# A spectral mixing and feed-forward kernel: its opening in a new order (w_in's first piece first, two products of w_in behind the last transform, w_out converted ahead of the first unit)

## Chip, cores, metric

One Trainium2 chip, one core of it. The metric is the device time of one launch in microseconds, median of several executions; lower is better. The runs were made in four sittings, on more than one chip, so kernels are compared by their ratio to the kernel before in the same sitting. The granted clock is the share of its full clock that TensorE was allowed in a stretch; "warm" stands for 1.00 and "cold" for 0.50. Engine names in the profile: PE is TensorE (matmul), PEld its weight loads, DVE is VectorE, ACT is ScalarE, POOL is GpSimd, SP is SyncE, which here issues DMAs only.

## The reference, cut to what matters

```python
x: (8, 3136, 256) float32
X = np.fft.fft(np.fft.fft(x, axis=1), axis=2).real       # mixing, over sequence and features
x = X.reshape(25088, 256)
h = x @ w_in                                             # 256 -> 1024
solu = h * softmax(h)
ln = (solu - mean) / sqrt(var + 1e-6) * g_ln
out = ln @ w_out                                         # 1024 -> 256
```

The weights arrive in float64 (eight bytes a number), so the kernel converts them itself, with integer operations on VectorE.

## The kernel before: the parts that matter here

The batch is worked off in four pairs. The first transform of a pair runs over pieces c = 0 to 7: two loads (xa straight, xb mirrored by an indirect DMA), an addition of the mirror and a fold on VectorE, four matmuls, a copy to z on ScalarE, a store of z to DRAM (zd). The turn reads zd back in another arrangement as g. Then 25 units per pair follow: a second transform, the up-product with w_in (L207), softmax work on VectorE and ScalarE, a block transpose, and four units later the down-product with w_out (L291). While a pair's units run, the next pair is loaded and transformed beside them. Only the first pair has nothing to hide behind: that is the opening.

```python
def turn(pr, i):
    pr.g[i] = gpool.tile([P, KG, D], FP32, tag="g", name="g")
    for j in range(4):
        k = j * NK + i * KG
        nc.gpsimd.dma_start(out=pr.g[i][j * NH : (j + 1) * NH, :, :],
                            in_=pr.zd[k : k + KG, :, :].rearrange("k n d -> n k d"))

# ... in Weights:
def load_out(self):                      # eight loads of 256 KB, float64
    ...
    for c in range(KF):
        load_piece(moe_w_out, self.raw[:, 2 * c * D : 2 * (c + 1) * D], Wo[:, c], c, 0, D)
    nc.vector.tensor_scalar(out=g_ln, in0=g_ln, scalar1=2.0 ** -20, scalar2=None, op0=ALU.mult)

def narrow_out(self, i):                 # a quarter of w_out to float32, times g_ln
    ...

def centre(self):                        # takes the mean over the 1024 rows out of w_out
    ...
    nc.scalar.mul(out=wbar, in_=cs, mul=1.0 / FF)
    for c in range(KF):
        nc.gpsimd.tensor_tensor(out=Wo[:, c, :], in0=Wo[:, c, :], in1=wbar, op=ALU.subtract)

def ahead(pr, step):                     # the next pair, beside unit `step`
    c, r = divmod(step - 2, 2)
    if step == 0:
        load(pr, 0)
        load(pr, 1)
    elif 0 <= c < NC:
        if r == 0:
            add_mirror(pr, c, nc.gpsimd)
        else:
            fold(pr, c)
            ...

# ... the opening:
for c in range(NC):
    add_mirror(first, c, nc.vector)
    fold(first, c)
    ...                                  # loads of later pieces
    for s in range(CH // 2):
        transform1(first, c * CH // 2 + s)
    if c < 4:
        weights.narrow_in(c)
    ...
    elif 3 < c < 7:
        weights.product_in(c - 4)
    if c == 5:
        weights.load_out()
weights.place_table()
turn(first, 0)
for i in range(2):
    weights.narrow_out(i)

# ... at the end of each unit i:
    if i < 2:
        weights.narrow_out(i + 2)
    elif i == 2:
        weights.centre()
    if 0 < i + 1 < NK // KG:
        turn(first, i + 1)
    if ahd:
        ahead(ahd, cur.k1)
```

The program's order is each engine's order: nothing is rearranged behind it.

## Time and profile before

| | us |
|---|---|
| median of the first 3 executions (of 4) | 1255.19 (1254.85) |
| the profiled execution, its span | 1256.66, 1254.8 |
| first product of the second transform (unit 0 begins) | 77.41 |
| first vector instruction of unit 0 ("even", L213) | 83.17 |
| first matmul after TensorE's last large gap (here called T) | 135.08 |
| TensorE busy from T to the end | all of it, but for 3 us near the end |

How to read it: TensorE has no slack after T, so all that the opening can do is to move T. The prediction below shows the lines for this.

### The profile page before, as it was taken

Reading aid. Unit: us, or ns where it says so; the run is one execution under the profiler, and the core shown is the slowest. Engines: PE = TensorE matmul, PEld = TensorE weight load, DVE = VectorE, ACT = ScalarE, POOL = GpSimd, SP = SyncE. Lnnn points to the kernel's source line nnn. Section 1 sums busy time; section 2 is a strip of 40 time slices with the busy share of each in tenths; the row PEclk is TensorE's granted clock in tenths of the full one; section 3 lists DMA queues with packets and bytes.
Section 4 is the critical chain, followed back from the end, with each engine's and each line's share of the span. In section 5 each row is a group of like instructions: output and inputs, shape, how many; then the busy total and the mean of one; then the engine's idle time right before and its main releaser. Section 6 shows DMA issues by size and latency. Waiting matters only on the chain.

```text
span 1254.8 us, 15771 instructions
## 1 busy us (share of the span) xinstructions
PE 1181.9 (94%) x4864; PEld 897.2 (72%) x4864; DVE 930.4 (74%) x1383; ACT 613.0 (49%) x1151; POOL 541.5 (43%) x964
## 2 busy tenths in 40 slices
PE   2746799999999999999999999999999999999997
PEld 1423587777777777877877778778777777777786
DVE  6748877877776887777776887787676787777760
ACT  1223554555554555545454555455454555555551
POOL 2014755444553555444453554553453333333331
PEclk9677899999999999999999999999999999999999
DMA  9636787675798676774697678866878464555643
GB/s 234 209 98 131 155 177 161 155 168 135 143 183 180 141 181 160 165 171 104 155 194 179 136 176 172 166 154 139 154 161 159 98 138 111 128 124 115 132 101 99
DMA packets 461971, 189.52 MB, mean 151 GB/s; under 512 B 430166, under 2 KB 443742, under 8 KB 461888
## 3 DMA queue, kind: packets, MB, share of 16 engines
q1 hardware_dynamic: 448064, 149.96, 56.8%
q0 software_dynamic: 13824, 38.55, 11.7%
q8 instruction: 40, 0.66, 0.2%
q14 instruction: 43, 0.35, 0.1%
HBM read 44.78 MB, written 38.80 MB: 67 GB/s over the span
## 4 chain that ended last, share of the span: by engine, by line
PE 89%; DVE 5%; DMA 2%; issue 1%; POOL 1%; ACT 1%; POOLq 0%; DVEq 0%; ACTq 0%; SPq 0%
PE ps_o L291 54%; PE ps_h L207 26%; PE ps L158 4%; PE ps L181 3%; PE ps L183 1%; DMA xb<-in_x_dram,idx 1%; DVE tmp L329 1%; POOL Wo L425 1%; DMA xa<-in_x_dram 0%; DVE h L221 0%; DVE tmp L342 0%; DVE u L240 0%; DMA raw_out<-in_moe_w_out_dram 0%; PE wps L403 0%; DVE y L119 0%
## 5 line engine op out<-in xcount | busy, mean ns | idle before, releaser
L291 PE MATMUL ps_o<-Wo,uT 128*128 128x256 f32 x3136 | 699.8, 381 | 2.9 <-DMA out_dram<-ot 2.9
L291 PEld LDWEIGHTS ps_o<-Wo,uT 128*128 128x128 f32 x3136 | 612.9, 197 | 66.0 <-issue 3.7
L207 PE MATMUL ps_h<-Wi,q 128*128 128x512 f32 x800 | 367.5, 603 | 12.7 <-DVE ev L213 11.8
L240 DVE SCALAR_TENSOR_TENSOR u<-h,u 128x1024 f32<-128x1024 f32 x196 | 233.6, 1228 | 140.0 <-ACT u L232 140.0
L232 ACT ACTIVATE u<-h,neg 128x1024 f32<-128x1024 f32 x196 | 223.5, 1141 | 205.4 <-DVE neg L226 192.2
L242 POOL TENSOR_SCALAR nmean<-usum 128x1 f32<-128x1 f32 x196 | 127.0, 649 | 385.0 <-DVE u L240 384.8
L249 ACT ACTIVATE h<-u,nmean 128x1024 f32<-128x1024 f32 x196 | 223.6, 1142 | 129.8 <-POOL nmean L242 129.8
L207 PEld LDWEIGHTS ps_h<-Wi,q 128*128 128x128 f32 x800 | 154.5, 194 | 165.6 <-issue 156.0
L221 DVE CUSTOM_DVE_ANT_0 h<-ev,ps_h 128x1024 f32<-128x1024 f32 x196 | 231.8, 1219 | 47.4 <-PE ps_h L207 39.5
L276 DVE STREAM_TRANSPOSE v<-u 128x1024 f32<-128x1024 f32 x200 | 238.1, 1231 | 0.1
L213 DVE SCALAR_TENSOR_TENSOR ev<-w_mid,q,ps_h 128x1024 f32<-128x1024 f32 x100 | 127.8, 1278 | 76.0 <-PE ps_h L207 72.7
L189 ACT COPY q<-ps 128x257 f32<-128x257 f32 x100 | 37.4, 374 | 219.4 <-PE ps L183 133.7
L303 POOL DMA_INDIRECT out_dram<-ot,idx x96 | 102.7, 1070 | 46.3 <-issue 22.4
L158 PE MATMUL ps<-y,F 98*100 98x258 f32 (+3 forms) x288 | 79.1, 411 | 36.3 <-DVE y L120 36.3
L181 PEld LDWEIGHTS ps<-T,g 128*128 128x128 f32 x400 | 60.7, 192 | 60.0 <-issue 60.0
L261 POOL TENSOR_SCALAR v<-ssq 128x2 f32<-128x2 f32 (+1 forms) x100 | 27.1, 271 | 169.4 <-ACT h L249 169.4
L296 ACT ACTIVATE ot<-ps_o,rs 128x256 f32<-128x256 f32 x196 | 80.9, 457 | 30.6 <-PE ps_o L291 30.6
L158 PEld LDWEIGHTS ps<-y,F 98*100 98x100 f32 x288 | 46.3, 184 | 50.7 <-DVE y L120 27.1
L264 POOL TENSOR_TENSOR rs<-v,neg_half 128x2 f32<-128x2 f32 (+1 forms) x100 | 72.4, 724 | 7.8
L181 PE MATMUL ps<-T,g 128*128 128x128 f32 x400 | 61.3, 276 | 12.4 <-DMA g<-zd 12.4
L170 POOL DMA_DIRECT2D g<-zd x80 | 48.0, 606 | 57.1 <-DMA xa<-in_x_dram 49.4
L161 ACT COPY z<-ps 100x512 f32<-100x512 f32 x64 | 36.2, 569 | 41.8 <-PE ps L158 26.8
(60 smaller groups left out, 480.6 us busy)
## 6 DMA issues: line engine op xcount, KB each, us to landing
uT<-v SPq DMA_DIRECT2D x784, 128.0 KB
zd<-z SPq DMA_DIRECT2D x32, 400.0 KB
g<-zd POOLq DMA_DIRECT2D x80, 160.0 KB, 5.5
out_dram<-ot SPq DMA_DIRECT2D x100, 128.0 KB
xa<-in_x_dram SPq DMA_DIRECT2D x28, 392.0 KB
raw_in<-in_moe_w_in_dram SPq DMA_DIRECT2D x4, 512.0 KB
raw_out<-in_moe_w_out_dram SPq DMA_DIRECT2D x8, 256.0 KB
uT<-v SPq DMA_DIRECT2D x32, 64.0 KB
```

Of the source, the lines that this page charges most:

```text
L158: nc.tensor.matmul(o[..., cs], F[:, 2 * t + h, :], i[..., cs], start=first, stop=True, skip_group_check=True)
L181: nc.tensor.matmul(ps[:, h * P : (h + 1) * P], g[:, k, h * P : (h + 1) * P], T[:, k1, :], start=(h == 0), stop=True, skip_group_check=True)
L207: nc.tensor.matmul(ps[:, fs], t.q[:, c * P : (c + 1) * P], Wi[:, c, fs], start=True, stop=True)
L213: nc.vector.scalar_tensor_tensor(out=t.ev, in0=w_mid, scalar=t.q[:, KD * P :], in1=ps, op0=ALU.mult, op1=ALU.add)
L221: nc.vector.tensor_tensor_reduce(out=t.h[s], in0=t.ev, in1=ps, scale=1.0, scalar=-3.0e38, op0=ALU.subtract if s else ALU.add, op1=ALU.max, ...
L232: nc.scalar.activation(out=t.u[s], in_=t.h[s], func=ACT.Exp, bias=t.neg[:, s : s + 1], accum_out=t.esum[:, s : s + 1])
L240: nc.vector.scalar_tensor_tensor(out=t.u[s], in0=t.h[s], scalar=1.0, in1=t.u[s], op0=ALU.mult, op1=ALU.mult, accum_out=t.usum[:, s : s + 1])
L242: nc.gpsimd.tensor_scalar(out=t.nmean[:, s : s + 1], in0=t.usum[:, s : s + 1], scalar1=-1.0 / FF, scalar2=None, op0=ALU.mult)
L249: nc.scalar.activation(out=t.h[s], in_=t.u[s], func=ACT.Square, bias=t.nmean[:, s : s + 1], accum_out=t.ssq[:, s : s + 1])
L276: nc.vector.transpose(out=t.batch.v[:, t.w, :, o], in_=t.u[s])
L291: nc.tensor.matmul(ps, uT[:, c, :, s], Wo[:, c, :], start=(c == 0), stop=(c == KF - 1))
L303: dma = nc.gpsimd.indirect_dma_start(out=out, out_offset=bass.IndirectOffsetOnAxis(ap=idx[:, i : i + 1], axis=0), in_=t.ot[s], in_offset=None)
```

## The change

Its intent is a shorter opening. VectorE idles for 8.6 us at the start; a conversion of w_in is put there. Two of three products of w_in go into the time in which z is stored and turned. w_out is loaded in one transfer and earlier, all four quarters of it are converted before unit 0, and its mean is taken out by one instruction on VectorE after unit 1 instead of eight on GpSimd after unit 2. The first turn is issued half by SyncE and half by GpSimd.

```diff
-    def turn(pr, i):
+    def turn(pr, i, engines=(nc.gpsimd,) * 4):
...
-            nc.gpsimd.dma_start(out=pr.g[i][j * NH : (j + 1) * NH, :, :],
+            engines[j].dma_start(out=pr.g[i][j * NH : (j + 1) * NH, :, :],
...
-            for c in range(KF):
-                load_piece(moe_w_out, self.raw[:, 2 * c * D : 2 * (c + 1) * D], Wo[:, c], c, 0, D)
+            if moe_w_out.dtype == FP32:
+                ...
+            else:
+                nc.sync.dma_start(out=self.raw.rearrange("p (c f) -> p c f", c=KF),
+                                  in_=moe_w_out.bitcast(I32).rearrange("(c p) f -> p c f", p=P))
...
-            for c in range(KF):
-                nc.gpsimd.tensor_tensor(out=Wo[:, c, :], in0=Wo[:, c, :], in1=wbar, op=ALU.subtract)
+            nc.vector.tensor_tensor(out=Wo, in0=Wo, in1=wbar.unsqueeze(1).to_broadcast([P, KF, D]), op=ALU.subtract)
...
+        weights.load_in()
+        weights.piece_in(0)
         load(first, 0)
         nc.sync.dma_start(out=F, in_=f_tab)
-        weights.load_in()
-        weights.piece_in(0)
         for c in range(1, 4):
+            weights.piece_in(c)
             load(first, c, rooms.get(c))
-            weights.piece_in(c)
-        weights.load_tables()
         for c in range(4, 6):
             load(first, c, rooms[c])
+        weights.load_tables()
...
         for c in range(NC):
+            if c < 4:
+                weights.narrow_in(c)
             add_mirror(first, c, nc.vector)
             fold(first, c)
             if c + 6 < NC:
                 load(first, c + 6)
+            if c == 1:
+                weights.load_table()
+            elif c == 3:
+                weights.load_out()
+                weights.mid()
+                weights.scale_out()
             for s in range(CH // 2):
                 transform1(first, c * CH // 2 + s)
-            ...
+            if c == 4:
+                weights.product_in(0)
+        turn(first, 0, (nc.sync, nc.gpsimd) * 2)
         weights.place_table()
-        turn(first, 0)
-        for i in range(2):
+        for h in range(1, 3):
+            weights.product_in(h)
+        for i in range(KF * D // NW):
             weights.narrow_out(i)
...
-            if i < 2:
-                weights.narrow_out(i + 2)
-            elif i == 2:
+            if i == 1:
                 weights.centre()
```

## The prediction

> **What bounds the kernel now.** I read the page's busy rows first, then the table by stages, then the chain of waits of the first 140 us, then each engine's timeline there. The busy rows (40 slices of 31.4 us, tenths) show two regimes:
>
> ```profile
> PE   2746799999999999999999999999999999999997
> PEclk9677899999999999999999999999999999999999
> DMA  9636787675798676774697678866878464555643
> ```
>
> TensorE is full from the sixth slice on; in the first five neither it nor its granted clock is. The stage table (window, length, busy of PE, PEld, DVE, ACT, POOL, clock, DMA share, GB/s) says the same:
>
> ```profile
> 94.10:125.50 31.40, 18.97 (x48) 10.16 (x49) 27.56 (x44) 10.48 (x20) 14.67 (x27) 0.78 0.69 131
> 157.00:188.00 31.00, 31.00 (x138) 24.82 (x138) 24.68 (x38) 16.69 (x31) 15.81 (x26) 1.00 0.82 177
> 400.00:800.00 400.00, 400.00 (x1690) 307.11 (x1688) 311.87 (x459) 212.57 (x403) 196.90 (x336) 1.00 0.72 161
> ```
>
> So from some point on the time is a fixed amount of TensorE work. TensorE's timeline gives the point: the last large idle time ends at 135.08 us, and the first down-product follows.
>
> ```profile
> 77.41 1.19 PE L181 MATMUL ps<-T,g 128*128 128x128 f32 x4 [12.42 <-DMA g<-zd]
> 135.08 2.03 PE L158 MATMUL ps<-y,F 98*100 98x258 f32 x4 [7.10 <-DVE y L120]
> ```
>
> From there to the end are 1254.8 - 135.1 = 1119.7 us, which the change does not touch. The change is worth exactly what it takes from these 135.1 us; being 2% faster would need 25.1 us of them, nearly a fifth.
>
> What sets 135.08, from the chain and the timelines:
>
> ```profile
> 2.85 10.30 DMA xb<-in_x_dram,idx
> 66.03 6.02 DMA xa<-in_x_dram
> 72.28 1.84 POOL g L170 x3
> 74.12 3.15 DMA g<-zd
> 122.43 6.48 POOL Wo L425 x8
> 128.91 2.32 POOL g L170 x4
> 131.25 2.37 POOL xa L127
> ```
>
> In order: (1) VectorE idles from 4.54 to 13.18 for the first mirrored piece of x, then alternates folds (2.5 us) and conversions of w_in (4.36 us, 15.71 to 20.07) without a gap to 49.9. (2) The last z is stored at 65.6, but the turn (z read back as g) starts only at 72.28 and has landed at 77.3. (3) Unit 0 starts; its first vector instruction, even, is at 83.17. (4) Units 0 and 1 each carry a quarter of w_out's conversion on VectorE, 91.85 to 96.38 and 106.27 to 110.77. (5) In unit 3 the eight subtractions on GpSimd (6.48 us) push back the next turn and the mirror of the next pair; the fold, and with it TensorE, waits for that.
>
> **What the Trainium skill says.** "DMA: Bandwidth & Descriptors", section Queues, rings and completion order: each DMA engine consumes one queue's descriptors in ring order and goes round between queues. The trace agrees with the order: w_out was issued from 55.3 and the z stores of 61.3 and 65.6 behind it were long in landing. The same page, Anatomy of one DMA, puts a fixed cost of about 2 us on a DMA, most of it the receipt of the write; here g lands 3.0 us after issue (median). "VectorE: DVE Perf Modes", section The perf-mode tier table: a float32 tensor_tensor of 2048 elements takes 2293 ns; the trace's 1020 elements took 1.22 us, which agrees. "TensorE: Matmul & The Clock Gate", The HAM clock gate: idle windows of about 3.4 us halve the clock; the table here shows 0.50 from 68 to 84 us, and unit 0's eight products of 128x512 took 6.25 us against 3.43 later.
>
> **The change part by part.**
>
> *w_in's first piece first.* Its conversion (4.36 us) moves into VectorE's 8.6 us of idle. The piece landed by 8.1 us even as the fourth load (the issue eight loads later waited for it till then), so as second load it is there by about 6. The mirrored piece comes from the other queue and should still land near 13.2. Folds 0 to 3 come at the same times as before, folds 4 to 7 4.4 us earlier. That does not reach the end in full: the z stores sit in one queue with all the loads. DMA is at 0.9 to 1.0 up to 36 us, and the z buffers (two) wait for stores: ScalarE waited until 39.88 for the first store. I add up the queue in its new order: store 0 landed at 40, then table T (0.82 MB, now ahead of store 1), stores 1 and 2 near 48, then w_out (2.1 MB, one transfer) to 56 at 260 GB/s, and store 3 behind it near 58. Each later pair of stores waits for the pair before it: 5 at 63, the last z is copied and store 7 issued at about 64. Before it was 65.6. **Gain about 1.5 us; most of the 4.4 is given back here.**
>
> *Products out of the loop.* One product stays inside, two (3.6 us each, 5 cold) go behind the last transform, in the time of the store and the turn. They would end near 70, about when g lands. Neutral for the path, but TensorE should be warmer.
>
> *The turn.* Store 7 took 6.7 us to be seen, behind the rest of w_out; with w_out long in I give it 3.5. The four issues on GpSimd (0.6 us each, 2.4) become two on each of two engines: 5.0 us for the turn become about 4. g is in at 64 + 3.5 + 4 = 71.5, against 77.3: **gain 5.8 us, the 1.5 included.**
>
> *w_out's conversion all ahead.* Four quarters at 4.55 us (60.68 to 65.27) are 18.2 us from about 57: done at 75.5. Unit 0's up-product can be ready at 71.5 + 5.3 = 76.8 (5.8 before, a little less on a warmer clock). The two paths are nearly level; even of unit 0 at **76.5 instead of 83.17, gain 6.7.**
>
> *Units 0 to 3.* Before: 83.17 to 135.08, 51.9 us. Away: two quarters, 9.0. Added: one subtraction of 2048 elements, about 2.3, on VectorE at the end of unit 1, and about 0.7 waiting for the mean (after ScalarE's squares). Away with GpSimd's 6.48: the wait of the fold (1.4) and the stretched vector work of unit 3 (1.75 instead of 1.23 each, some 1.4 in all). 51.9 - 9.0 + 3.0 - 2.8 = 43.1. VectorE still sets the pace here, 10.0 us a unit.
>
> Sum: TensorE is continuous from about 76.5 + 43.1 = 119.6, **15.5 us earlier**; I take off 0.3 for small gaps in the first full units. 1255.2 - 15.2 = **1240.0 us, 1.2% faster**.
>
> **The rivals.**
> 1. *The z chain swallows it.* w_out as one transfer of 2.1 MB lies ahead of five stores; if they, or T, cost 3 to 5 us more than I add up, the turn is as late as before. Then only the 9.0 + 2.8 - 3.0 = 8.8 of the units are left: 1246. For it: the DMA share in the opening, and the wait to 39.88. Against it: all the bytes had to pass before the turn in any case.
> 2. *VectorE becomes the bound before unit 0.* If w_out lands at 60 instead of 56, the conversion ends at 79 and even is late by 2.5: 1242.5. For it: the two paths are level.
> 3. *The whole sum arrives, and a warm clock more.* If w_out does not delay the stores and TensorE enters unit 0 warm, even could come at 73: 1236. It cannot come much sooner, as 18.2 us of conversion have to follow the last fold at 52 to 55.
> 4. *All hidden.* If TensorE were short of nothing but its own work from the start, nothing would come of it. Against it: 7.10 us of idle just before 135.08 and 12.42 before 77.41.
>
> **Range and chances.** Rivals 1 and 3 give 1246 and 1236; with a margin of 1 to 2 us for what I do not see, the range is 1234 to 1247. Faster by over 2% needs 25.1 us: even 73 together with units of 38 us, for which I see no source; 0.04. Slower by over 2% would need a new wait of 40 us; 0.01. Within 2%: 0.95.
>
> **What would show it.** Right: the first conversion on VectorE before 10 us; the last z store issued near 64; g landed near 71; conversion of w_out ending near 75; no vector work but the units' own and one subtraction of about 2.3 us in units 0 to 3; TensorE without gaps from about 120; the rest about 1120 us as before. Wrong: z stores that wait longer behind w_out; VectorE waiting for Q or g_ln, which are now loaded later; a subtraction that waits several us for the mean; gaps after 120 because the shuffled blocks of the first batch are not there; or a steady pace other than before.

## The result, and the profile after

The changed kernel is correct and takes 1249.55 us (median of 4, 1248.44 to 1250.45) against 1254.85 of the kernel before in the same rounds: ratio 0.9955, 95% interval 0.9938 to 0.9972. The gain is about 5.5 us; 15.2 had been forecast, and 1249.55 lies above the range.

The busy rows of the changed kernel's page (40 slices of 31.2 us, tenths). TensorE is full one slice earlier, from the fifth on; the fourth, in which units 1 to 3 run, reaches only four tenths:

```profile
PE   2774999999999999999999999999999999999997
PEclk9988999999999999999999999999999999999999
DMA  9828886775898776765798678776878464655543
```

TensorE's timeline at the two places shown before (start, duration, engine, line, operation, idle time and what ended it):

```profile
77.38 1.19 PE L181 MATMUL ps<-T,g 128*128 128x128 f32 x4 [5.70 <-DMA g<-zd]
127.37 2.03 PE L158 MATMUL ps<-y,F 98*100 98x258 f32 x4 [7.30 <-DVE y L120]
```

Unit 0 begins at 77.38 us; before, it was 77.41. The whole new opening has moved it by nothing. T has moved by 7.7 us, from 135.08 to 127.37, so all of that was gained inside units 0 to 3. From T to the end are 1118.9 us (1119.7 before), as foreseen.

The chain of waits of the changed kernel in that stretch (start, duration, what):

```profile
38.57 11.59 DMA zd<-z
...
51.36 7.07 DMA zd<-z
...
59.62 3.62 DMA zd<-z
...
64.44 4.15 DMA zd<-z
...
69.39 0.67 POOL g L170
70.06 6.97 DMA g<-zd
...
101.47 2.29 DVE Wo L429
...
117.44 2.60 DVE neg L226
```

The z stores follow one another as worked out, within about 2 us, and the last is issued at 64.44 (forecast: about 64). Then comes the line that the prediction lacks: a turn that needs 6.97 us to land, where 3.15 had been seen. SyncE's queue in the changed kernel shows what else went out then:

```profile
68.77 0.80 SPq L170 DMA_DIRECT2D g<-zd  x2
69.67 0.80 SPq L105 DMA_DIRECT2D xa<-in_x_dram  x2
```

and the DMA queues from 71 to 73 us (queue, packets, MB, share of the 16 engines) show who had the engines. q1 is SyncE's queue; it had moved 0.33 MB, SyncE's half of the turn, by 71 us, so of the turn only GpSimd's half on q0 was still missing.

```profile
q1 hardware_dynamic: 119, 0.36, 64.7%
q0 software_dynamic: 37, 0.12, 23.2%
```

Two suspects followed from this. **Traffic theory:** the next pair's first two loads of x (0.8 MB, emitted at the end of unit 0, but with nothing in front of them on SyncE but the turn itself) crowd GpSimd's half of the turn. **Port theory:** VectorE now converts w_out during the turn, and keeps GpSimd from writing its DMA descriptors (the entries that tell a DMA engine what to move). I held the second to be the likelier, because the Trainium skill describes such a case ("SBUF — State Buffer", section SBUF: two separate sides: while VectorE runs an operation in a two-port mode, the descriptors of a GpSimd DMA cannot be written). The page says so of two-port modes only, and in which mode the conversion ran was not established.

### The profile page after: what moved, and what is told of

Its sections match the earlier page's. It is cut to its first block, busy times and chain, and to the rows that moved or that the text cites. A ratio compares the mean times of both kernels' runs of the same rounds, so it can differ in the third digit from the quotient of the medians.

```text
span 1246.3 us, 15757 instructions
## 1 busy us (share of the span) xinstructions
PE 1181.9 (95%) x4864; PEld 897.7 (72%) x4864; DVE 933.8 (75%) x1384; ACT 612.5 (49%) x1151; POOL 534.8 (43%) x954
## 4 chain that ended last, share of the span: by engine, by line
PE 89%; DMA 6%; DVE 3%; ACT 1%; issue 1%; POOL 0%; SPq 0%; POOLq 0%; ACTq 0%; DVEq 0%
PE ps_o L291 54%; PE ps_h L207 27%; PE ps L158 4%; PE ps L181 3%; DMA Q<-in_q_tab_dram 2%; DMA zd<-z 2%; PE ps L183 1%; DMA raw_in<-in_moe_w_in_dram 1%; DVE h L221 1%; DVE u L240 1%; DMA g<-zd 1%; DVE v L276 0%; ACT u L232 0%; DMA out_dram<-ot,idx 0%; DVE ev L213 0%
## 5 line engine op out<-in xcount | busy, mean ns | idle before, releaser
L291 PEld LDWEIGHTS ps_o<-Wo,uT 128*128 128x128 f32 x3136 | 612.6, 197 | 65.6 <-issue 3.4
```

The lines of the kernel that those rows point to most:

```text
L291: nc.tensor.matmul(ps, uT[:, c, :, s], Wo[:, c, :], start=(c == 0), stop=(c == KF - 1))
```

## The experiments

Twelve runs of eleven kernels were made (x_late and x_late_timed are one kernel), all correct. "First product", "even" and T are read from each kernel's own trace, one execution each; two traces of one kernel, x_late and x_late_timed, have T 2.0 us apart.

| kernel | turn issued | first product | even | T | last product ends | span | time, median (n) | ratio to before |
|---|---|---|---|---|---|---|---|---|
| before | 72.28 | 77.41 | 83.17 | 135.08 | 1250.1 | 1254.8 | 1254.85 (4) | 1 |
| changed | 68.77 | 77.38 | 83.11 | 127.37 | 1241.8 | 1246.3 | 1249.55 (4) | 0.9955 |
| turn_sync | 68.64 | 73.83 | 78.72 | 123.01 | 1237.3 | 1248.5 | 1251.05 (6) | 0.9959 |
| turn_pool | 72.11 | 77.45 | 83.21 | 127.69 | 1242.4 | 1247.0 | 1248.78 (1) | |
| half_ahead | 68.26 | 77.22 | 82.99 | 136.23 | 1250.2 | 1254.8 | 1256.84 (4) | 1.0004 |
| x_late | 67.66 | 72.31 | 75.67 | 120.22 | 1234.4 | 1239.0 | 1240.96 (1) | |
| x_late_timed | 68.12 | 72.92 | 77.70 | 122.22 | 1236.3 | 1240.9 | 1245.53 (5) | 0.9916 |
| before_late | 69.81 | 75.00 | 80.77 | 132.12 | 1247.0 | 1251.6 | 1254.59 (4) | 0.9990 |
| x_late_pool | 68.97 | 74.17 | 79.09 | 123.62 | 1238.0 | 1242.7 | 1244.43 (1) | |
| x_late_sync | 67.37 | 72.26 | 78.02 | 122.73 | 1237.3 | 1248.5 | 1250.48 (1) | |
| x_late_wout | 68.64 | 73.62 | 79.39 | 125.06 | 1239.9 | 1244.5 | 1246.22 (1) | |
| x_late_gcentre | 67.91 | 72.75 | 76.97 | 121.08 | 1236.4 | 1240.9 | 1243.00 (1) | |
| x_late_oldorder | 69.10 | 73.92 | 78.95 | 123.53 | 1238.1 | 1242.7 | 1245.51 (4) | 0.9920 |
| best | 68.56 | 73.68 | 76.96 | 120.26 | 1234.3 | 1238.9 | 1241.39 (4) | 0.9887 |

In every row the last product ends 1114 to 1115 us after T: that TensorE's work from T on is fixed, the first step of the prediction, holds throughout.

### Traffic or port?

**x_late**: the next pair's x is held back by a small write (one element per partition) that VectorE makes at the end of unit 0.

```diff
-            load(pr, 0)
-            load(pr, 1)
+            load(pr, 0, hold=pr.p == 1)
+            load(pr, 1, hold=pr.p == 1)
# in load():
+        if hold:
+            nc.vector.memset(xa[:, 0:1, 0:1], 0.0)
         nc.sync.dma_start(out=xa, ...)
```

> The changed kernel, with the next pair's two x loads held back by a one-element write on VectorE at the end of unit 0 (about 91 us), so that no other load runs beside the first turn; the result stays right. Traffic theory: g lands 4 to 5 us after the issue, near 73, and the time falls by about 4 to 1245. Port theory: GpSimd's half still lands at 76 or later, time within 1.5 us of the changed kernel's 1249.5.

**half_ahead**: only two quarters of w_out ahead of unit 0, so that VectorE is idle during the turn.

```diff
-        for i in range(KF * D // NW):
+        for i in range(2):
             weights.narrow_out(i)
...
-            if i == 1:
+            if i < 2:
+                weights.narrow_out(i + 2)
+            elif i == 2:
                 weights.centre()
```

> The changed kernel, with only half of w_out converted ahead of unit 0 and a quarter each in units 0 and 1, as before the change (the mean is taken out after unit 2). VectorE is idle from about 66 on, so during the whole turn. Port theory: GpSimd's half of the turn is undisturbed and g lands near 73.5, even of unit 0 at about 79, although the time as a whole gets worse (9 us of conversion are back in the units): about 1252 to 1254. Traffic theory: g still lands near 77 and the time is about 1257.

GpSimd's issues in x_late, VectorE's conversion beside them, and the chain behind them:

```profile
68.28 1.29 POOL L172 DMA_DIRECT2D g<-zd  x2 [45.48 <-DMA zd<-z]
```

```profile
68.97 0.88 DVE L354 SCALAR_TENSOR_TENSOR Wo<-raw_out,g_ln,tmp 128x256 f32<-128x256 f32 x2
```

```profile
68.95 3.01 DMA g<-zd
```

The same of half_ahead; VectorE's first instruction after 65.6 us shows that it had been idle for 17.42 us:

```profile
68.88 1.29 POOL L170 DMA_DIRECT2D g<-zd  x2 [45.63 <-DMA zd<-z]
```

```profile
82.99 1.28 DVE L213 SCALAR_TENSOR_TENSOR ev<-w_mid,q,ps_h 128x1024 f32<-128x1024 f32 x1 [17.42 <-PE ps_h L207]
```

```profile
69.54 7.23 DMA g<-zd
```

This decides it, against my guess. With VectorE idle and the x loads there, the turn's last transfer took 7.23 us to land; with VectorE busy and the x loads gone, 3.01. The two issues on GpSimd took 1.29 us in both. The port theory falls as the cause of the late turn; the traffic theory stands. The time of half_ahead shows another thing: without the two quarters moved ahead, nothing is left of the gain that the timing could show (ratio 1.0004, interval 0.9989 to 1.0019). With the turn held up as it was, the gain came from that step.

**turn_pool** and **turn_sync**: the four transfers all on GpSimd, or all on SyncE.

```diff
-        turn(first, 0, (nc.sync, nc.gpsimd) * 2)
+        turn(first, 0)                       # turn_pool
+        turn(first, 0, (nc.sync,) * 4)       # turn_sync
```

> The changed kernel with all four transfers of the first turn on GpSimd, as before the change; VectorE still converts w_out until about 75. Port theory: twice the descriptors have to be written against VectorE, so g lands later than in the changed kernel, about 79 (most of it once VectorE is free at 75.4), time about 1251. Traffic theory: four issues of 0.6 us and 0.8 MB of x beside them; g lands at about 77 as in the changed kernel, time 1249 to 1250.

> The changed kernel with all four transfers of the first turn issued by SyncE, none by GpSimd. In the changed kernel the turn was issued at 68.8 us and had landed only at 77.0, 8.3 us later. Port theory (GpSimd's writing of descriptors is held up by VectorE's conversion of w_out): with no GpSimd issue left, g lands about 3.7 us after the first issue, near 72.5, unit 0's even on VectorE is near 76 to 77 instead of 83.1, and the time is about 1243 (6 to 7 us less than the changed kernel). Traffic theory (the next pair's two x loads, 0.8 MB, crowd the turn): g is ahead of x on the one queue here, so it also lands early; this run does not tell the two apart, it tells both from a third, that the turn takes 8 us whoever issues it (then 1249 to 1250).

In turn_pool the first product came at 77.45, in the changed kernel at 77.38. With nothing on SyncE to wait for the last z store, the x loads went out at once at 65.8, and the turn started only at 72.11. In the changed kernel half of the turn is on SyncE and the x loads come behind that half; the turn starts earlier, but GpSimd's half lands later. The 0.8 MB have to pass either before the turn or beside it: from 69 to 77 us the changed kernel's DMA engines moved 1.46 MB, the turn's 0.64 and the x loads' 0.8. So the first product stands at 77.4 in the kernel before, in the changed one and in this one alike; with x held back it comes at 75.00, 72.31 and 74.17 (before_late, x_late, x_late_pool). The Trainium skill agrees ("DMA: Bandwidth & Descriptors", section Issuing engines are not separate DMA queues: transfers of several engines end up on the same 16 DMA engines). In turn_sync all of the turn lies ahead of x in one queue, and the first product is 3.6 us earlier, as both theories said. Its time did not follow:

```profile
core 0 of [0], span 1248.5 us
...
1238.12 0.96 POOL L303 DMA_INDIRECT out_dram<-ot,idx  x1 [8.76 <-ACT ot L296]
```

The last store is issued at 1238.12, and the span ends 10.4 us later; in the changed kernel and in all rows with a GpSimd transfer in the first turn that distance is 3.7 to 3.9 us. What the gain was at the front, it lost at the very end.

**x_late_sync** was run to see whether that comes with the two GpSimd transfers fewer.

```diff
-        turn(first, 0, (nc.sync, nc.gpsimd) * 2)
+        turn(first, 0, (nc.sync,) * 4)       # on x_late
```

> x_late with all four transfers of the turn on SyncE. The kernel with all four on SyncE but x not held back finished its last product 4.5 us earlier than the changed kernel and yet took as long, because the program ended 9.4 us after the issue of the last store instead of 2.9. If that end goes with the two GpSimd transfers fewer, it appears here as well: last product at about 1235, end of the span near 1246, time about 1247. If it was something else: end near 1239, time 1241.

It does: again 10.4 us (1238.14 to 1248.5). The mechanism behind these 6.6 us stays open; the profile shows no instruction in them, and no packet of a transfer.

### What the x loads cost before the change, and how x_late times

**before_late**: the kernel before, with the same hold and nothing else.

```diff
-            load(pr, 0)                      # on the kernel before, as in x_late
+            load(pr, 0, hold=pr.p == 1)
```

> The kernel before, with only the next pair's two x loads held back to the end of unit 0. If those loads cost the opening already before the change (the last z store is issued at 65.6 us, they are issued right behind it at 66.0, and the turn starts only at 72.28 when they have landed): the turn starts near 69.5 to 70, g lands near 75, and the time is 2 to 3 us below the kernel before. If instead the z store was slow because of the rest of w_out in front of it, as the prediction had it: turn at 72, g at 77, time unchanged.

Its turn starts at 69.81 instead of 72.28, and T is 3.0 us earlier in the trace. So the last z store, which the prediction took to be slow "behind the rest of w_out", was seen 2.5 us late because of the x loads right behind it: held back, they leave it 3.6 us, about the 3.5 that the prediction allowed it. In time the gain is 1.3 us by the ratio 0.999, interval 0.9975 to 1.0005: not clear of nothing.

**x_late_timed** is x_late in five rounds.

> The same kernel as x_late (the changed kernel with the next pair's x held back to the end of unit 0), now timed. Traffic theory: the single time of 1240.96 holds, 1241 within 1.5, ratio to the kernel before 0.988. If that single run was luck: 1249, ratio 0.9955.

Ratio 0.9916 (0.9903 to 0.9930): some 5 us better than the changed kernel (0.9955), but 1245.5, not 1241. The two traces differ by 2.0 us in T, and all of it is there at unit 0's even already. Unit 0's eight up-products in x_late, then in x_late_timed:

```profile
73.58 3.70 PE L209 MATMUL ps_h<-Wi,q 128*128 128x512 f32 x8 [0.46 <-ACT q L191]
```

```profile
74.18 5.13 PE L209 MATMUL ps_h<-Wi,q 128*128 128x512 f32 x8 [0.46 <-ACT q L191]
```

TensorE had idled 1.44 us before unit 0 in the first and 2.72 us in the second, and the granted clock fell to 0.50 in the second only. The single run was a lucky one: its clock over the whole span was 0.989, those of the five timed executions 0.984 to 0.986. (It ran on another chip too, but the kernel before took about the same there, 1256.7 us against 1256.3.) The trace of x_late_timed is of its fastest execution, 1243.05; where the other four lost 2 to 3 us more, no trace shows.

**x_late_pool**: x_late, the turn undivided on GpSimd.

```diff
-        turn(first, 0, (nc.sync, nc.gpsimd) * 2)
+        turn(first, 0)                       # on x_late
```

> x_late with all four transfers of the turn on GpSimd (the split of the turn undone). Traffic theory with the issue times seen so far: turn issued at 68.2, four issues of 0.65 us instead of two, landing 3.0 us after the last but one: g near 73.9 instead of 72.0, TensorE a little later and perhaps cold, time 1243. If the split is worth nothing here: 1241.

From the turn's first issue to the first product are 5.2 us, against 4.65 and 4.8 in the two traces of x_late. But the first issue is not the same moment: GpSimd starts 0.8 us after the last z store has been seen, SyncE 0.2. From the store (seen at 68.18 here, at 67.48 and 67.95 in x_late) to the first product are 6.0 us, against 4.8 and 5.0. So with the traffic gone the split is worth about 1 us in these traces, as the prediction had it; the single time cannot resolve it.

### The other steps of the prediction, one by one, on x_late

**x_late_oldorder**: the loads and the conversions of w_in in the order of before.

```diff
-        weights.load_in()
-        weights.piece_in(0)
         load(first, 0)
         nc.sync.dma_start(out=F, in_=f_tab)
+        weights.load_in()
+        weights.piece_in(0)
         ...                                  # piece and x swapped, tables ahead of x 4 and 5
         for c in range(NC):
-            if c < 4:
-                weights.narrow_in(c)
             add_mirror(first, c, nc.vector)
             fold(first, c)
+            if c < 4:
+                weights.narrow_in(c)
```

> x_late with the order of the loads and of w_in's conversions as before the change (x first, conversion behind the fold). Folds 4 to 7 then come 4.4 us later on VectorE. If the z stores' queue gives that back, as the prediction had it (1.5 us left): last z store issued at 65 to 66 instead of 64, time 1 to 2 us above x_late_timed, 1246.5 to 1247.5. If the 4.4 us count in full: 1250. If nothing: 1245.5.

1245.51 and ratio 0.9920, against 1245.53 and 0.9916 with the new order. The chain of waits of x_late_oldorder has the last stores here:

```profile
60.24 3.85 DMA zd<-z
...
65.29 3.64 DMA zd<-z
```

The last is issued at 65.29, against 63.87 in x_late: 1.4 us, where VectorE had been given 4.4. The first product comes 1.0 us later than in x_late_timed. So the step that gave the change its name saves about one microsecond in the traces, and none that the timing resolves (the two intervals leave 2 to 3 us either way).

**x_late_wout**: w_out's transfer on ScalarE's queue.

```diff
-                nc.sync.dma_start(out=self.raw.rearrange("p (c f) -> p c f", c=KF),
+                nc.scalar.dma_start(out=self.raw.rearrange("p (c f) -> p c f", c=KF),
```

> x_late with w_out's one transfer issued on ScalarE's queue instead of SyncE's, so that the z stores do not stand in line behind it. If w_out in front of them is what holds the z stores (in the changed kernel store 3 was issued at 51.4 and seen at 58.4): the last z is stored 2 to 4 us earlier (60 to 62 instead of 64), g lands near 69. w_out itself lands later than 56.9, at 58 or so, so VectorE's conversion ends at 75 to 76 and is then the bound: even at 76 to 77, time as x_late within 2 us.

A miss: the last z store was issued at 64.33, not at 60 to 62. The conversion did end later (76.4), and T was 125.06. A second queue did not let the stores past w_out, and TensorE, after waiting 4.72 us for them, ran its transforms slowly (16 matmuls took 6.57 us, most of it at a granted clock of 0.50). From 44 to 52 us the DMA engines were busy for 0.90 or more of each 2 us, which fits w_out holding the stores by its bytes; this run alone does not settle it.

**x_late_gcentre**: the mean taken out on GpSimd, after unit 1.

```diff
-            nc.vector.tensor_tensor(out=Wo, in0=Wo, in1=wbar.unsqueeze(1).to_broadcast([P, KF, D]), op=ALU.subtract)
+            for c in range(KF):
+                nc.gpsimd.tensor_tensor(out=Wo[:, c, :], in0=Wo[:, c, :], in1=wbar, op=ALU.subtract)
```

> x_late with the mean taken out of w_out by eight subtractions on GpSimd, as before the change, but still after unit 1. By the prediction's working VectorE is spared 2.3 us plus 0.5 of waiting, but GpSimd's 6.5 us lie in front of its part of unit 2 (turn, means): unit 2's squares wait 3 to 4 us, so even to the first transform of the next pair takes 45 to 46 us instead of 44.5. If the subtraction on GpSimd were hidden there: 41.7 us.

Another miss: from even to T are 44.1 us, against 44.5 with VectorE. Where the subtraction runs makes no difference of note. Unit 2's vector work stretches instead, as two products of 1.22 us become 1.75 while GpSimd subtracts, and one of unit 3 becomes 3.68 beside GpSimd's mirror.

**best**: x_late with three idle products behind the last product of w_in, to keep TensorE's clock, and with the next pair's first mirror on VectorE.

```diff
+        warm = ps_m.tile([P, NW], FP32, tag="m", name="warm")
+        for _ in range(3):
+            nc.tensor.matmul(warm, ones, weights.w_in[1][:, 0:NW], start=True, stop=True)
...
-                add_mirror(pr, c, nc.gpsimd)
+                add_mirror(pr, c, nc.vector if pr.p == 1 and c == 0 else nc.gpsimd)
```

> x_late with two additions: three idle products of 128x512 on TensorE behind the last product of w_in, so that its clock does not fall before unit 0 (their result is not used), and the next pair's first mirror on VectorE instead of GpSimd (in the changed kernel VectorE's small negation in unit 3 took 2.59 us while that mirror ran on GpSimd). Clock theory: unit 0's eight up-products take 3.7 us in most executions, even is at 75.7 to 76, TensorE is continuous from about 119, time 1239 to 1240, 4 us below x_late_timed's 1245.5. If the clock before unit 0 is not what makes the executions of x_late differ: 1243 to 1244.

TensorE's timeline of best:

```profile
71.11 2.74 PE L503 MATMUL warm<-w_in,ones 128*128 128x512 f32 x6
73.68 0.61 PE L183 MATMUL ps<-T,g 128*128 128x128 f32 x4
...
74.87 3.70 PE L209 MATMUL ps_h<-Wi,q 128*128 128x512 f32 x8 [0.47 <-ACT q L191]
```

The idle products cost twice what I had meant (2.74 us, six passes), but unit 0 enters warm: 3.70 us for the up-products, even 3.3 us after the first product instead of 4.8 in x_late_timed and 5.7 in the changed kernel. The profile shows no wait of TensorE for g here, so some of the idle products may stand in front of unit 0; the time is 1.4 us above the 1239 to 1240 that was expected. From even to T are 43.3 us instead of 44.5. The time is 1241.39, ratio 0.9887 (0.9870 to 0.9903): 14 us better than before, the best of all that ran. Its four executions have a mean granted clock of 0.987 to 0.989 over the whole span, those of x_late_timed 0.984 to 0.986. By the ratios some 3.6 us lie between the two; how they divide between the idle products and the mirror was not timed apart.

## Why the prediction was wrong

The prediction named the fixed work from T on, the place of unit 0's even as the sum to watch, and the units' own saving. The first held, the last came within 1.2 us; even did not come earlier at all. Even was forecast for 76.5 and came at 83.11, 6.6 us late: g landed 5.5 us late, from g to even took 0.8 us more, and 0.3 are a slip in the sum (it finds 71.5 + 5.3 = 76.8 and goes on with 76.5). Point by point:

- **"The turn" is the step that failed.** It says: "Store 7 took 6.7 us to be seen, behind the rest of w_out; with w_out long in I give it 3.5", and "5.0 us for the turn become about 4". The store took 4.15 us, and the turn 8.3 us from its first issue to landing (68.77 to 77.03) instead of 4: that is 4.3 of the 5.5 us. The next pair's x loads, which had stood in the chain of the kernel before as the line of 66.03 and which the prediction itself shows, were left out of the new sum. Before, they delayed the start of the turn; after, they ran beside it. Without them the turn, split as in the change, lands 4.3 to 4.6 us after its first issue (x_late: 67.66 to 71.96). The forecast of 4 was near for a turn alone; the step left out what runs beside it.
- **"Unit 0's up-product can be ready at 71.5 + 5.3 ... a little less on a warmer clock."** It was 5.7 us. The late g left TensorE idle for 5.70 us, the clock fell as it had before the change, and the eight products took 5.46 us. The late g follows from the first point, and in these traces the cold clock came with every wait of 2.00 us or more; x_late shows 3.4 us from first product to even when TensorE stays warm, and 4.8 when not.
- Together these make even 83.11 instead of 76.5. With the two causes taken away it came at 76.96 in best and 75.67 in the first run of x_late: the forecast of 76.5 was a fair sum of a path that the change alone does not reach.
- **"z stores" and "most of the 4.4 is given back here"**: right. Last store at 64.44 against about 64; x_late_oldorder shows 1.4 us of 4.4 left. But it was not the stores alone that gave it back, as the step has it: fold 4 came only 2.1 us earlier than before, not 4.4 (its last instruction at 41.52 against 43.66). The first mirrored piece landed 0.6 us later (13.78 against 13.18), and VectorE waited for Q, which one of the prediction's signs of being wrong had named:

```profile
38.53 0.48 DVE L394 TENSOR_SCALAR w_mid<-ones,Q 128x128 f32<-128x128 f32 x2 [1.40 <-DMA Q<-in_q_tab_dram]
```

- **"w_out's conversion all ahead"**: four quarters, forecast 57 to 75.5, measured 56.9 to 75.35. The two paths would have been level; they were not, because the turn was late.
- **Units 0 to 3**: forecast 43.1, measured 44.26. The subtraction took 2.29 us and waited 0.50, as said. Mis-sized is the "stretched vector work" that was to go with GpSimd's subtractions: a new stretch of 2.4 us came instead, VectorE's negation beside GpSimd's mirror.

```profile
117.44 2.59 DVE L226 TENSOR_SCALAR neg<-nmax 128x2 f32<-128x2 f32 x1
```

```profile
117.64 2.36 POOL L127 TENSOR_TENSOR xa<-xa,xb 98x1020 f32<-98x1020 f32 x1
```

  The negation of 128x2 ends with the mirror; alone it takes 0.17. With that mirror on VectorE (best), the units take 43.3.
- **The base of the subtraction.** T = 135.08 was read from an execution of 1256.66 us, and the gain was taken from a median of 1255.2. The profiled execution of the changed kernel, in turn, was its fastest. So the traces show 8.5 us between the two spans, and the medians 5.3. Some 2 to 3 us of a forecast of this kind are lost in which execution was profiled.

Of the rivals, the first came nearest in its size (1246, "the turn is as late as before"), and for a reason that it did not name: not the z stores but the transfers behind them.

## What to carry to other kernels

When a change moves a transfer, list everything else that its queue and the DMA engines will have to do in the new window, also loads for a much later stage that an in-order issuing engine lets out as soon as it is free; a load that nothing needs for 40 us can take 5 us from one that everything waits for, and a tiny write that it depends on (0.07 us here) holds it back. Before crediting a step with the work that it moves, ask whether the queue behind it takes the gain back (4.4 us of VectorE's idle time bought 1.4 us of earlier stores). And check a suspicion from a manual by a run in which only that suspect is idle: here it was not the cause.

## What the Trainium skill lacked or had wrong

- "SBUF — State Buffer", SBUF: two separate sides: the page has GpSimd's descriptor writing locked out while VectorE runs a two-port operation. Whether the conversion's instructions are such was not established; the runs show no lockout of any size beside them: two issues took 1.29 us with VectorE converting (x_late) and with VectorE idle (half_ahead), four took 2.64 us with it converting (turn_pool) and 2.42 with it idle (before). Where both engines compute, a stretch did show: a negation of 0.17 us took 2.59 beside a mirror on GpSimd.
- No page that I read has it: a kernel whose first turn had no GpSimd transfer ended 10.4 us after the issue of its last store, in both kernels of that kind, instead of 3.7 to 3.9.
- "DMA: Bandwidth & Descriptors", Queues, rings and completion order: the section gives no figure for what loads issued right behind a store of the same queue do to it. Here the last z store was seen 2.5 us later with two x loads behind it (turn at 72.28 against 69.81 in before_late).
- "TensorE: Matmul & The Clock Gate", The HAM clock gate: the clock is said to fall after an idle window of about 3.4 us. Here it fell to 0.50 after shorter gaps, each followed by about 0.8 us of short products: 2.00 us (x_late_gcentre, at 75.0 us), 2.25 (x_late_oldorder) and 2.72 (x_late_timed); after 1.44 (x_late) it did not.
